# One gather per block: x, its gate and the dense output of a token share one row in DRAM

## The chip, the cores and the metric

The kernel runs on one core of a Trainium2 chip. The metric is the time of one execution on the device in microseconds (us). Five engines work side by side: TensorE (PE in the profile, its weight loads PEld), VectorE (DVE), ScalarE (ACT), GpSimd (POOL) and SyncE (SP), and 16 DMA engines move data for them.

## The reference

Two layers follow each other. The first is a block-sparse attention, the second a mixture of experts with a dense layer beside it.

```
# attention: 4 batches, 8 heads, 768 tokens, head size 64
k_min, k_max = min, max of k over chunks of 32 keys
ub   = sum(max(q*k_min, q*k_max));  causal chunks only
keep the 6 chunks with the highest ub for each query
x    = softmax(masked q k^T / 8) v          # -> 3072 tokens x 512
# experts: 8 of them, each with two 512 x 512 matrices
y_dense = relu(x @ w1_dense) @ w2_dense
logits  = x @ w_gate;  e = argmax(logits);  g = softmax(logits)[e]
out     = y_dense + g * (relu(x @ w1[e]) @ w2[e])
```

## The kernel before

**Attention, with the dense layer between.** The 16 pairs of heads (4 batches of 4 pairs) go through one after another. SP loads k, q and v three pairs ahead (`load`, L257), POOL casts them to f16, TensorE makes scores and the product with v, ACT the exponentials, POOL the masks on the diagonal. The result of a batch stands in `xbig`, in SBUF, as f16 rows of 528 elements for each token: 512 of x, two that hold the gate as one f32, and padding. When a batch is ready, its part of the dense layer (`batch_fills`, L172) is dealt out between the attention's steps of the next batch: `xtr` transposes x, `gate` (L185) makes the logits, the argmax and the gate's reciprocal sum and stores the batch's rows to the DRAM tensor `xd` (L206), `l1` and `l2` are the two layers, and `l2` stores 128 tokens of the dense output, as f32 rows of 2048 bytes, to the DRAM tensor `yd` (L231). Both stores are on SP's queue. The last batch's dense layer runs after the attention.

**Routing.** After the last gate the kernel computes for each token its place in a list sorted by expert (L446 to L509). The list is cut into 31 blocks of 128 places, each with one expert, and padded at the ends of experts. `gi` holds the token of each place for the gather, `si` the same for the scatter, with an index out of bounds for padding. The offset of each block's expert within the weights is loaded to TensorE's registers (L512).

**The expert stage.** A block goes through these steps:
- `gather(i)` (L520): POOL issues two indirect DMAs, 128 rows of `xd` (1056 bytes each) to the tile `xg`, and 128 rows of `yd` (2048 bytes each) to `yg`.
- `tx(i)` (L529): TensorE transposes x of the block (four 128 x 128 pieces), DVE copies the result to `exT`.
- `e1(i)` (L537): four matmuls with the expert's first matrix, ACT's relu to `eh`.
- `th(i)` (L546): four transposes of `eh`, ACT copies to `ehT`.
- `e2(i)` (L554): four matmuls with the second matrix; DVE makes `yo` = product x gate + dense output (L561), reading `xg` and `yg`; POOL issues an indirect DMA that scatters `yo` to the rows of `out` (L562).

`xg`, `yg` and `yo` come from the pool `eg` with three buffers each, so the gather of block i + 3 waits until the `yo` of block i has been computed, which is the last to read its `xg` and `yg`. Gathers are written two blocks ahead. A scatter writes to `out`, of which it isn't known which rows it hits, so each scatter waits until the one before it has landed. For the same reason a gather waits for every store to the tensor that it reads.

The order of instructions on each engine is fixed when the program is built, by a scheduler that works from the order in the source; each engine then takes its instructions in that order. The trace shows the order that came out: on POOL gather of x, gather of y, scatter, and on TensorE the second layer of a block in every other block split in two around the next `tx`.

Of the kernel before, what the change touches and what calls it, by code (L numbers as in the profile page):

```python
# [8 lines left out]
FP = mybir.dt.float32  # L9
BF = mybir.dt.bfloat16  # L10
HF = mybir.dt.float16
AF = mybir.ActivationFunctionType
ALU = mybir.AluOpType
# [4 lines left out]
def kernel(  # L18
# [12 lines left out]
    nc = tc.nc  # L31
    B, H, S, D = q.shape
    NT = S // 128
    NC = S // 32
    N, Dm = out.shape
# [6 lines left out]
    NP = B * HP  # L42
    NBLK = NM + E - 1
    XW = Dm + 16
    U16 = mybir.dt.uint16

    const = ctx.enter_context(tc.tile_pool(name="const", bufs=1))
    dram = ctx.enter_context(tc.tile_pool(name="dram", bufs=1, space=bass.MemoryType.DRAM))

    xd = dram.tile([N, XW], U16, name="xd")  # L50
    yd = dram.tile([N, Dm], FP, name="yd")

    ident = const.tile([128, 128], HF)
    make_identity(nc, ident)
# [55 lines left out]

    xbig = const.tile([128, NM, XW], HF)
    nc.gpsimd.memset(xbig[:, :, Dm:XW], 0.0)

# [30 lines left out]
    for u, un in enumerate(units):  # L144
        o = 0
# [13 lines left out]
    def evac(dst, src):  # L159
        evac_turn[0] += 1  # L160
        if evac_turn[0] % 2:
            nc.vector.tensor_copy(dst, src)
        else:
            nc.scalar.copy(dst, src)
# [3 lines left out]
    def ptile(kind, shape, dt, name):  # L168
        pool, tag = cur[kind]
        return pool.tile(shape, dt, name=name, tag=tag)  # L170

    def batch_fills(b):  # L172

        xT = mx.tile([128, NK, S], HF, name="xT")
        out_list = []

        def xtr(mi):
            def f():
                tp = ptile("tr", [128, NK, 128], HF, "tp")
                for ko in range(NK):  # L180
                    nc.tensor.transpose(tp[:, ko], xbig[:, b * NT + mi, ko * 128 : (ko + 1) * 128], ident)
                nc.vector.tensor_copy(xT[:, :, mi * 128 : (mi + 1) * 128], tp)
            return f

        def gate():  # L185
            lg = ptile("tr", [128, NT, E], FP, "lg")
            for mi in range(NT):
                for ko in range(NK):
                    nc.tensor.matmul(lg[:, mi], xT[:, ko, mi * 128 : (mi + 1) * 128], wg[:, ko],
                                     start=(ko == 0), stop=(ko == NK - 1))  # L190
            mxv = mg.tile([128, NT], FP, name="mxv")
            nc.vector.tensor_reduce(out=mxv, in_=lg, op=ALU.max, axis=mybir.AxisListType.X)
            dl = mg.tile([128, NT, E], FP, name="dl")
            nc.vector.tensor_tensor(dl, lg, mxv.unsqueeze(2).to_broadcast([128, NT, E]), ALU.subtract)
            el = mg.tile([128, NT, E], FP, name="el")
            nc.scalar.activation(el, dl, AF.Exp)
            cand = mg.tile([128, NT, E], FP, name="cand")
            nc.vector.scalar_tensor_tensor(cand, dl, 0.0, iom8, ALU.is_ge, ALU.mult)
            mn = mg.tile([128, NT], FP, name="mn")
            nc.vector.tensor_reduce(out=mn, in_=cand, op=ALU.min, axis=mybir.AxisListType.X)  # L200
            nc.vector.tensor_tensor(ohp[:, :, 1 + b * NT : 1 + (b + 1) * NT].rearrange("p e t -> p t e"),
                                    iom8, mn.unsqueeze(2).to_broadcast([128, NT, E]), ALU.is_equal)
            ss = mg.tile([128, NT, 1], FP, name="ss")
            nc.vector.tensor_reduce(out=ss, in_=el, op=ALU.add, axis=mybir.AxisListType.X)
            nc.vector.reciprocal(xbig[:, b * NT : (b + 1) * NT, Dm : Dm + 2].bitcast(FP), ss)
            nc.sync.dma_start(out=xd[b * S : (b + 1) * S].rearrange("(m p) w -> p m w", p=128),  # L206
                              in_=xbig[:, b * NT : (b + 1) * NT].bitcast(U16))

        G = 3

        def l1(g, j, hold):
            def f():
                if j == 0:
                    hold["h"] = mh.tile([128, NK, G * 128], HF, name="hT")
                hp = ptile("h", [128, G * 128], FP, "hp")
                for ko in range(NK):
                    nc.tensor.matmul(hp, wd[:, ko, j * 128 : (j + 1) * 128], xT[:, ko, g * G * 128 : (g + 1) * G * 128],  # L217
                                     start=(ko == 0), stop=(ko == NK - 1))
                nc.scalar.activation(hold["h"][:, j], hp, AF.Relu)  # L219
            return f  # L220

        def l2(g, i, hold):
            def f():
                yp = ptile("y", [128, Dm], FP, "yp")
                for j in range(NK):
                    nc.tensor.matmul(yp, hold["h"][:, j, i * 128 : (i + 1) * 128], wd[:, NK + j],  # L226
                                     start=(j == 0), stop=(j == NK - 1))
                ys = my.tile([128, Dm], FP, name="ys")
                evac(ys, yp)
                m = b * NT + g * G + i  # L230
                nc.sync.dma_start(out=yd[m * 128 : (m + 1) * 128], in_=ys)  # L231
            return f

        for mi in range(NT):
            out_list.append(xtr(mi))
        out_list.append(gate)
        dense = []
        for g in range(NT // G):
            hold = {}
            for j in range(NK):  # L240
                dense.append(l1(g, j, hold))
            for i in range(G):
                dense.append(l2(g, i, hold))
        return out_list, dense

    with (
# [10 lines left out]
        def load(p):  # L257
            b, hp = divmod(p, HP)
            for nm, src in (("k", k), ("q", q), ("v", v)):
                f = aload.tile([128, 2, NT, D], FP, name=nm + "f")  # L260
                st[p][nm] = f
                for g in range(2):
                    nc.sync.dma_start(out=f[:, g], in_=src[b, 2 * hp + g].rearrange("(t p) d -> p t d", p=128))

        def cast(p):
            s = st[p]
# [108 lines left out]
        for kind in ("tr", "h", "y"):  # L375
            cur[kind] = (pfill, "fb")
        load(0)
        load(1)
        load(2)
        load_dense()  # L380
# [15 lines left out]
        for i, (p, u) in enumerate(seq):  # L396
# [24 lines left out]
            if u == NU - 1:  # L421
                norm(p)
                if p % HP == HP - 1 and p + 1 < NP:
                    a, d = batch_fills(p // HP)
# [4 lines left out]
    with (  # L429
# [2 lines left out]
        tc.tile_pool(name="p3", bufs=2, space=bass.MemoryType.PSUM) as p3,  # L432
        tc.tile_pool(name="p4", bufs=1, space=bass.MemoryType.PSUM) as p4,
        tc.tile_pool(name="rt", bufs=1) as rt,
        tc.tile_pool(name="eg", bufs=3) as eg,
        tc.tile_pool(name="et", bufs=2) as et,
    ):
        cur.update(tr=(p1, "tr"), h=(p2, "h"), y=(p3, "y"))
# [2 lines left out]
        a, d = batch_fills(B - 1)  # L441
# [62 lines left out]
        gi = rt.tile([128, NBLK], mybir.dt.int32)  # L504
# [3 lines left out]
        si = rt.tile([128, NBLK], mybir.dt.int32)  # L508
# [10 lines left out]

        def gather(i):  # L520
            s = es[i]
            s["x"] = xg = eg.tile([128, XW], U16, name="xg")
            nc.gpsimd.indirect_dma_start(out=xg, out_offset=None, in_=xd,  # L523
                                         in_offset=bass.IndirectOffsetOnAxis(ap=gi[:, i : i + 1], axis=0))
            s["y"] = yg = eg.tile([128, Dm], FP, name="yg")
            nc.gpsimd.indirect_dma_start(out=yg, out_offset=None, in_=yd,  # L526
                                         in_offset=bass.IndirectOffsetOnAxis(ap=gi[:, i : i + 1], axis=0))

        def tx(i):  # L529
            s = es[i]  # L530
            tp = p1.tile([128, NK, 128], HF, name="tp", tag="tr")
            for ko in range(NK):
                nc.tensor.transpose(tp[:, ko], s["x"][:, ko * 128 : (ko + 1) * 128].bitcast(HF), ident)  # L533
            s["xT"] = xT = et.tile([128, NK, 128], HF, name="exT")
            nc.vector.tensor_copy(xT, tp)  # L535

# [17 lines left out]
        def e2(i):  # L554
            s = es[i]
            yp = p3.tile([128, Dm], FP, name="yp", tag="y")
            for j in range(NK):
                nc.tensor.matmul(yp, s["hT"][:, j], wef[:, bass.ds(offs[i] + (NK + j) * 512, 512)],  # L558
                                 start=(j == 0), stop=(j == NK - 1))
            o = eg.tile([128, Dm], FP, name="yo")  # L560
            nc.vector.scalar_tensor_tensor(o, yp, s["x"][:, Dm : Dm + 2].bitcast(FP), s["y"], ALU.mult, ALU.add)  # L561
            nc.gpsimd.indirect_dma_start(out=out, out_offset=bass.IndirectOffsetOnAxis(ap=si[:, i : i + 1], axis=0),  # L562
                                         in_=o, in_offset=None, bounds_check=N - 1, oob_is_err=False)

        gather(0)
        gather(1)
        tx(0)
        for i in range(NBLK):
            e1(i)
            if i + 2 < NBLK:  # L570
                gather(i + 2)
            if i + 1 < NBLK:
                tx(i + 1)
            if i > 0:
                e2(i - 1)
            th(i)
# [31 lines left out]
```

## Time and profile before

| what | value |
|---|---|
| time, median of 2 runs | 397.26 us (395.28 and 399.24) |
| profiled execution | 394.51 us, of which its span is 392.8 us |
| PE busy | 258.8 us, 66% of the span, 2426 matmuls |
| DVE, ACT busy | 192.1 us, 159.7 us |
| POOL busy | 208.0 us, 53% |
| DMA | 56.92 MB, mean 145 GB/s |

The span is the time from the first to the last instruction that the profiler recorded; the rest of the execution lies around it. A busy share over the whole span mixes the attention (up to about 235 us) with the expert stage, so the stages have to be read apart.

### The profile page before, as it was taken

The page shows a single profiled execution, that of the slowest core. Times are in us where ns is not written, and L with a number is a line of the kernel's source. Part 1 is how long each engine was busy: PE and PEld are TensorE (multiplying, and loading weights), DVE is VectorE, ACT ScalarE, POOL GpSimd, SP SyncE. Part 2 cuts the span into 40 slices and gives each one's busy share as a digit, 9 for nine tenths or more (in the row PEclk, how much of TensorE's full clock was granted, in tenths as well). Part 3 has the DMA queues.
Part 4 walks back from the last instruction along what each step waited for, and adds up shares of the span by engine and source line. Part 5 has one row for each costly group of instructions (what it writes and reads, how often), then busy time and mean ns, then how long its engine had stood idle before and what let it go on. Part 6 is the DMA issues. An engine that isn't in the chain of part 4 may idle for free. (4 is left out here: it accounts for less than half of the span.)

```text
span 392.8 us, 7052 instructions
## 1 busy us (share of the span) xinstructions
PE 258.8 (66%) x2426; PEld 152.8 (39%) x2426; DVE 192.1 (49%) x538; ACT 159.7 (41%) x303; POOL 208.0 (53%) x370
## 2 busy tenths in 40 slices
PE   0157377157599989999898872667555658565660
PEld 0135254045365666666665531333222323222230
DVE  8284438248387798777952890222222323232220
ACT  1016257056276867787675320322132222322230
POOL 9946185174455555554322025366756656666541
PEclk9998869779699999999999996888989996989895
DMA  9999999999997886211031425143444444444440
GB/s 182 208 222 214 208 204 198 170 199 204 222 236 191 190 200 145 94 53 56 3 119 49 164 106 173 42 154 114 131 133 132 149 145 135 134 136 133 128 121 0
DMA packets 98370, 56.92 MB, mean 145 GB/s; under 512 B 78462, under 2 KB 90750, under 8 KB 98336
## 3 DMA queue, kind: packets, MB, share of 16 engines
q1 hardware_dynamic: 81856, 28.42, 32.8%
q0 software_dynamic: 16480, 28.06, 30.1%
q8 instruction: 20, 0.33, 0.3%
q14 instruction: 14, 0.11, 0.1%
HBM read 50.08 MB, written 17.66 MB: 172 GB/s over the span
## 5 line engine op out<-in xcount | busy, mean ns | idle before, releaser
L334 ACT ACTIVATE ex<-sp 128x512 f16<-128x512 f32 (+1 forms) x176 | 91.7, 585 | 63.1 <-PE sp L330 31.1
L344 POOL TENSOR_SCALAR_AFFINE_SELECT ex<-ex 128x128 f16<-128x128 f16 (+1 forms) x176 | 52.2, 306 | 55.9 <-ACT ex L334 53.0
L362 PE MATMUL op<-v,ex 128*128 128x65 f16 x672 | 47.6, 200 | 34.6 <-POOL ex L344 29.7
L330 PE MATMUL sp<-r,kT 128*128 128x512 f16 (+3 forms) x256 | 65.1, 328 | 3.6 <-ACT ex L334 2.1
L362 PEld LDWEIGHTS <-ex 128*128 128x128 f16 x672 | 37.3, 101 | 49.5 <-POOL ex L344 35.0
L535 DVE COPY exT<-tp 128x512 f16<-128x512 f16 x31 | 13.2, 425 | 80.5 <-PE tp L533 59.3
L523 POOL DMA_INDIRECT xg<-xd,gi x31 | 30.3, 977 | 41.5 <-DVE yo L561 21.6
L552 ACT COPY ehT<-tp 128x512 f16<-128x512 f16 x31 | 18.2, 586 | 74.2 <-PE tp L550 67.9
L541 PE MATMUL hp<-we,exT 128*128 x124 | 37.4, 432 | 10.2 <-DVE exT L535 5.8
L558 PE MATMUL yp<-we,ehT 128*128 x124 | 38.8, 419 | 4.5 <-ACT ehT L552 2.6
L533 PE MATMUL tp<-ident,xg 128*128 128x128 f16 x124 | 14.2, 247 | 40.7 <-DMA xg<-xd,gi 40.7
L562 POOL DMA_INDIRECT out_dram<-yo,si x31 | 31.5, 1015 | 15.3 <-issue 13.4
L561 DVE SCALAR_TENSOR_TENSOR yo<-yp,xg,yg 128x512 f32<-128x512 f32 x31 | 23.3, 750 | 31.9 <-PE yp L558 27.2
L526 POOL DMA_INDIRECT yg<-yd,gi x31 | 29.4, 949 | 10.5 <-issue 10.2
L322 DVE COPY r<-pp 128x768 f16<-128x768 f16 x32 | 17.0, 554 | 32.8 <-PE pp L320 32.6
L544 ACT ACTIVATE eh<-hp 128x512 f16<-128x512 f32 x31 | 18.5, 597 | 35.2 <-PE hp L541 26.3
L533 PEld LDWEIGHTS <-xg 128*128 128x128 f16 x124 | 8.3, 108 | 56.9 <-DMA xg<-xd,gi 56.8
L217 PE MATMUL hp<-xT,wd 128*128 128x384 f16 x128 | 26.5, 325 | 0.7 <-ACT hT L219 0.3
L330 PEld LDWEIGHTS <-kT 128*128 128x128 f16 x256 | 21.8, 103 | 11.1 <-issue 8.2
L226 PE MATMUL yp<-wd,hT 128*128 128x512 f16 x96 | 24.6, 378 | 1.5 <-DVE xbig L371 1.0
L269 POOL CAST q<-qf 128x768 f16<-128x768 f32 x16 | 13.3, 831 | 21.5 <-DMA qf<-in_q_dram 20.9
L294 ACT ACTIVATE qp<-pp 128x768 f16<-128x768 f16 x16 | 13.0, 810 | 23.1 <-PE pp L292 23.1
(115 smaller groups left out, 431.0 us busy)
## 6 DMA issues: line engine op xcount, KB each, us to landing
we<-in_moe_w_dram POOLq DMA_DIRECT2D x16, 512.0 KB
kf<-in_k_dram SPq DMA_DIRECT2D x32, 192.0 KB, 4.4
qf<-in_q_dram SPq DMA_DIRECT2D x32, 192.0 KB, 4.5
vf<-in_v_dram SPq DMA_DIRECT2D x32, 192.0 KB, 4.7
yd<-ys SPq DMA_DIRECT2D x24, 256.0 KB, 2.1
xd<-xbig SPq DMA_DIRECT2D x4, 792.0 KB, 4.3
wd<-in_moe_w_dense_dram POOLq DMA_DIRECT2D x2, 512.0 KB
xg<-xd,gi POOLq DMA_INDIRECT x31
```

The costliest lines, as they stand in the source:

```text
L217: nc.tensor.matmul(hp, wd[:, ko, j * 128 : (j + 1) * 128], xT[:, ko, g * G * 128 : (g + 1) * G * 128], start=(ko == 0), stop=(ko == NK - 1))
L226: nc.tensor.matmul(yp, hold["h"][:, j, i * 128 : (i + 1) * 128], wd[:, NK + j], start=(j == 0), stop=(j == NK - 1))
L330: nc.tensor.matmul(sp[:, o : o + z - a], kT[p % NB][g][:, bb * 128 : (bb + 1) * 128], s["r", g][:, a:z], start=(o == 0), stop=True, skip_g ...
L334: nc.scalar.activation(ex[:, :o], sp[:, :o], AF.Exp, scale=0.125)
L344: nc.gpsimd.affine_select(out=exd, in_=exd, compare_op=ALU.is_ge, fill=0.0, base=0, pattern=[[0, n], [1, 128]], channel_multiplier=-1)
L362: nc.tensor.matmul(op[:, g, t * (D + 1) : (t + 1) * (D + 1)], ex[:, c : c + 128], v16[p % NB][:, g, bb, :], start=(u == g and n == 0), sto ...
L523: nc.gpsimd.indirect_dma_start(out=xg, out_offset=None, in_=xd, in_offset=bass.IndirectOffsetOnAxis(ap=gi[:, i : i + 1], axis=0))
L526: nc.gpsimd.indirect_dma_start(out=yg, out_offset=None, in_=yd, in_offset=bass.IndirectOffsetOnAxis(ap=gi[:, i : i + 1], axis=0))
L541: nc.tensor.matmul(hp, s["xT"][:, ko], wef[:, bass.ds(offs[i] + ko * 512, 512)], start=(ko == 0), stop=(ko == NK - 1))
L558: nc.tensor.matmul(yp, s["hT"][:, j], wef[:, bass.ds(offs[i] + (NK + j) * 512, 512)], start=(j == 0), stop=(j == NK - 1))
L561: nc.vector.scalar_tensor_tensor(o, yp, s["x"][:, Dm : Dm + 2].bitcast(FP), s["y"], ALU.mult, ALU.add)
L562: nc.gpsimd.indirect_dma_start(out=out, out_offset=bass.IndirectOffsetOnAxis(ap=si[:, i : i + 1], axis=0), in_=o, in_offset=None, bounds_c ...
```

## The change

The row of a token in `xd` grows to 3104 bytes: first 2048 bytes of the dense output as f32, then the 1056 bytes of x and gate as before. `yd` goes away: `l2` stores to the first part of `xd`'s rows, `gate` to the second. `gather` issues one indirect DMA per block for the whole row, and `tx` and the computation of `yo` read their parts of it. `eg` has four buffers in place of three, and gathers run three blocks ahead in place of two, with three before the loop. Each scatter is declared to be independent of the other scatters, so it no longer waits until the one before has landed. The loads of k, q and v take their pieces from a view over two heads; the elements and their number per DMA are the same.

```diff
+    RW = 2 * Dm + XW
-    xd = dram.tile([N, XW], U16, name="xd")
-    yd = dram.tile([N, Dm], FP, name="yd")
+    xd = dram.tile([N, RW], U16, name="xd")
...
-            nc.sync.dma_start(out=xd[b * S : (b + 1) * S].rearrange("(m p) w -> p m w", p=128),
+            nc.sync.dma_start(out=xd[b * S : (b + 1) * S, 2 * Dm :].rearrange("(m p) w -> p m w", p=128),
...
-                nc.sync.dma_start(out=yd[m * 128 : (m + 1) * 128], in_=ys)
+                nc.sync.dma_start(out=xd[m * 128 : (m + 1) * 128, 0 : 2 * Dm], in_=ys.bitcast(U16))
...
+                sv = src[b, 2 * hp : 2 * hp + 2].rearrange("g (t p) d -> p g t d", p=128)
                 for g in range(2):
-                    nc.sync.dma_start(out=f[:, g], in_=src[b, 2 * hp + g].rearrange("(t p) d -> p t d", p=128))
+                    nc.sync.dma_start(out=f[:, g], in_=sv[:, g])
...
-        tc.tile_pool(name="eg", bufs=3) as eg,
+        tc.tile_pool(name="eg", bufs=4) as eg,
...
-            s["x"] = xg = eg.tile([128, XW], U16, name="xg")
+            s["x"] = xg = eg.tile([128, RW], U16, name="xg")
             nc.gpsimd.indirect_dma_start(out=xg, out_offset=None, in_=xd,
-                                         in_offset=bass.IndirectOffsetOnAxis(ap=gi[:, i : i + 1], axis=0))
-            s["y"] = yg = eg.tile([128, Dm], FP, name="yg")
-            nc.gpsimd.indirect_dma_start(out=yg, out_offset=None, in_=yd,
                                          in_offset=bass.IndirectOffsetOnAxis(ap=gi[:, i : i + 1], axis=0))
...
-                nc.tensor.transpose(tp[:, ko], s["x"][:, ko * 128 : (ko + 1) * 128].bitcast(HF), ident)
+                nc.tensor.transpose(tp[:, ko], s["x"][:, 2 * Dm + ko * 128 : 2 * Dm + (ko + 1) * 128].bitcast(HF), ident)
...
-            nc.vector.scalar_tensor_tensor(o, yp, s["x"][:, Dm : Dm + 2].bitcast(FP), s["y"], ALU.mult, ALU.add)
-            nc.gpsimd.indirect_dma_start(out=out, out_offset=bass.IndirectOffsetOnAxis(ap=si[:, i : i + 1], axis=0),
+            nc.vector.scalar_tensor_tensor(o, yp, s["x"][:, 3 * Dm : 3 * Dm + 2].bitcast(FP), s["x"][:, 0 : 2 * Dm].bitcast(FP), ALU.mult, ALU.add)
+            sc = nc.gpsimd.indirect_dma_start(out=out, out_offset=bass.IndirectOffsetOnAxis(ap=si[:, i : i + 1], axis=0),
                                          in_=o, in_offset=None, bounds_check=N - 1, oob_is_err=False)
+            if i:
+                tc.declare_no_dep(sc.ins, group="scatter", reason="each scatter writes rows of its own")
+            tc.add_to_no_dep_group("scatter", sc.ins)
 
         gather(0)
         gather(1)
+        gather(2)
         tx(0)
         for i in range(NBLK):
             e1(i)
-            if i + 2 < NBLK:
-                gather(i + 2)
+            if i + 3 < NBLK:
+                gather(i + 3)
```

## Rows read from the trace of the kernel before

**Rows 1.** The page's part 2: busy tenths in 40 slices of 9.8 us, POOL.
```profile
POOL 9946185174455555554322025366756656666541
```

**Rows 2.** The windows: attention (0 to 210) and the expert stage (250 to 380).
```profile
0.00:210.00 210.00, 146.49 (x1766) 99.36 (x1767) 137.38 (x409) 114.44 (x223) 114.38 (x273) 0.93 0.85 167
...
250.00:380.00 130.00, 82.06 (x456) 37.66 (x454) 33.41 (x57) 33.53 (x57) 82.34 (x84) 0.91 0.43 135
```

**Rows 3.** Groups by line in 255 to 393 us, POOL's three.
```profile
L562 POOL DMA_INDIRECT out_dram<-yo,si x30 | 30.4, 1015 | 15.0 <-issue 13.1 <-DMA out_dram<-yo,si 1.9
L523 POOL DMA_INDIRECT xg<-xd,gi x27 | 26.3, 975 | 27.2 <-DVE yo L561 14.1 <-issue 6.2 <-DMA out_dram<-yo,si 4.5
L526 POOL DMA_INDIRECT yg<-yd,gi x27 | 25.6, 948 | 8.2 <-issue 7.9 <-DMA out_dram<-yo,si 0.3
```

**Rows 4.** The list of waits in 250 to 393 us: total, times, longest.
```profile
PE tp L533 <- DMA xg<-xd,gi: 36.5, 24, 2.6
...
POOL xg L523 <- DVE yo L561: 21.6, 9, 7.5
```

**Rows 5.** The tile yo: min/median/max ns, first and last start.
```profile
L561 DVE SCALAR_TENSOR_TENSOR yo<-yp,xg,yg x31: 742/751/753, 250.0 to 383.0; 128x512 f32<-128x512 f32 x31
```

**Rows 6.** The timeline in 254 to 275 us: start, duration, what, idle before.
```profile
254.50 0.40 PE L533 MATMUL tp<-ident,xg 128*128 128x128 f16 x4 [2.58 <-DMA xg<-xd,gi]
...
255.50 1.87 PE L541 MATMUL hp<-we,exT 128*128 x4 [0.38 <-DVE exT L535]
...
259.22 1.02 PE L541 MATMUL hp<-we,exT 128*128 x4
259.52 0.59 ACT L552 COPY ehT<-tp 128x512 f16<-128x512 f16 x1 [1.52 <-PE tp L550]
...
260.25 1.02 PE L558 MATMUL yp<-we,ehT 128*128 x4
...
261.31 0.75 DVE L561 SCALAR_TENSOR_TENSOR yo<-yp,xg,yg 128x512 f32<-128x512 f32 x1 [1.47 <-PE yp L558]
...
268.38 0.75 DVE L561 SCALAR_TENSOR_TENSOR yo<-yp,xg,yg 128x512 f32<-128x512 f32 x1 [0.43 <-issue]
...
269.40 0.98 POOL L523 DMA_INDIRECT xg<-xd,gi  x1 [1.88 <-DVE yo L561]
...
270.68 0.95 POOL L526 DMA_INDIRECT yg<-yd,gi  x1 [0.30 <-issue]
...
272.27 0.40 PE L533 MATMUL tp<-ident,xg 128*128 128x128 f16 x4 [1.66 <-DMA xg<-xd,gi]
...
272.50 0.39 PE L550 MATMUL tp<-ident,eh 128*128 128x128 f16 x4
...
273.27 1.02 PE L541 MATMUL hp<-we,exT 128*128 x4 [0.38 <-DVE exT L535]
...
274.39 0.60 ACT L544 ACTIVATE eh<-hp 128x512 f16<-128x512 f32 x1 [0.82 <-PE hp L541]
```

**Rows 7.** The timeline at the stage's start, 235 to 244 us.
```profile
235.14 1.06 POOL L523 DMA_INDIRECT xg<-xd,gi  x1 [6.20 <-PE yp L226]
235.25 1.06 SPq L231 DMA_DIRECT2D yd<-ys  x2
...
238.62 0.61 PE L533 MATMUL tp<-ident,xg 128*128 128x128 f16 x4 [3.31 <-DMA xg<-xd,gi]
...
240.08 0.96 POOL L526 DMA_INDIRECT yg<-yd,gi  x1 [1.32 <-issue]
...
243.92 3.57 PE L541 MATMUL hp<-we,exT 128*128 x8 [3.26 <-issue]
```

**Rows 8.** The line L512 on TensorE's queue: the load of the experts' offsets.
```profile
L512 PEldq TENSOR_LOAD <-eo x1: 2802/2802/2802, 240.9 to 240.9; - x1
```

**Rows 9.** The timeline at the end, 383 to 393 us.
```profile
383.00 0.75 DVE L561 SCALAR_TENSOR_TENSOR yo<-yp,xg,yg 128x512 f32<-128x512 f32 x1 [1.31 <-PE yp L558]
...
386.37 0.98 POOL L562 DMA_INDIRECT out_dram<-yo,si  x1 [1.88 <-issue]
```

## The prediction

> **What bounds the kernel now.** I read the share of busy time over the span first [rows 1], to cut it into stages. Up to about 235 us the attention and the dense layer run; there POOL's digits fall to nearly nothing and then stand at 5 to 7 until the end. The windows [rows 2] put numbers to this: in 250 to 380 us POOL is busy 82.3 of 130 us, TensorE 82.1, DVE and ACT 33 each, and the DMA engines 43% at 135 GB/s. No engine is full, so the stage waits in a circle, and the change lies in this circle alone.
>
> The rate first: the 31 `yo` run from 250.0 to 383.0 us [rows 5], so a block costs 133.0 / 30 = 4.43 us. POOL's groups [rows 3] say what it does with that: gathers of xg 0.975, of yg 0.948, scatter 1.015 us, each behind 0.30 us between two issues of POOL [rows 6]: 3 x 0.30 + 2.94 = 3.84 us of 4.43. The list of waits [rows 4] names the rest. TensorE waits 36.5 us for xg to land, and the gather of xg waits 21.6 us for `yo`, which frees its buffer. So two limits lie close together: POOL's queue (3.84 us) and the loop through three buffers. I worked this loop out from the timeline [rows 6]: `yo` ends at 269.13, the gather starts at 269.40 and takes 0.98, its rows are used by `tx` at 272.27 (1.89 us later), `tx` to the end of `eh` is 274.99 - 272.27 = 2.72 us, then a handover of about 0.2, `th` 0.39, another 0.2, and from `ehT` to the end of `yo` 262.06 - 259.52 = 2.54. In all 0.27 + 0.98 + 1.89 + 6.05 = 9.19 us. Three blocks share one turn: 3 x 4.43 = 13.3 us. The other 4.1 us of the turn are POOL's and TensorE's queues and the slow clock.
>
> The clock belongs to it: the first layer of a block takes 1.87 us after TensorE idled 2.58 us, and 1.02 us in other blocks [rows 6], the two levels of 1.2 and 2.4 GHz; over the stretch the granted clock is 0.91 [rows 2]. Each long wait for a gather is thus paid again in slow matmuls.
>
> **The change part by part.**
>
> *One gather for two.* POOL loses one instruction per block. The trace has no gather of 3104-byte rows, so its price is bounded: 1056-byte rows cost 0.975, 2048-byte rows 0.948 [rows 3], so the price doesn't grow with the row, and I take 0.98. The upper bound is the two together with their gap, 2.22, if a longer row were to be issued as two pieces; lower than 0.95 I see no reason for. POOL per block then: 0.98 + 1.015 + 0.60 = 2.59 us (upper bound 3.84 as now).
>
> *Landing.* The bytes don't change: 128 x (3104 + 2048) = 660 KB per block. At 135 GB/s the engines are 43% busy, which makes some 314 GB/s if they were full, 2.1 us per block: no bound at any rate that I forecast. But `tx` must now wait for all of the row, 262 KB more, an estimate of 262 / 314 = 0.83 us, at best nothing, when both parts overlap in flight. The Trainium skill (DMA: Bandwidth & Descriptors, section Anatomy of one DMA, SWDGE path) gives 2.0 us plus the bytes over 436 GB/s for a DMA of this kind. By that the merged gather takes 2.91 us against 2.31 for xg alone, 0.6 us more instead of 0.83; for xg the rows have 2.87 us from the start of the issue to the use (269.40 to 272.27, [rows 6]), so the page's size is about right here. By the page the turn below would be 0.2 us shorter, 0.06 us per block.
>
> *Four buffers instead of three,* and a gather three blocks ahead. The turn becomes 9.19 + 0.83 = 10.02 us over four blocks: 2.5 us per block with no queueing, and 14.1 / 4 = 3.5 with all the 4.1 us of today's. The most of these hang on the cause that goes (xg behind yg and a scatter in POOL's queue, the slow clock), so this isn't the likeliest end.
>
> *TensorE.* With its data there and the fast clock, a block is `tx` and `th` together 0.62 us (272.27 to 272.89), 1.02 for each layer: 2.66 us, plus the 0.38 us in which the first layer waits for `exT` [rows 6] where nothing lies between: 3.04. That is above POOL's 2.59 and the loop's 2.5. So TensorE becomes late next. I take 3.1 us per block, bounds 2.66 (no gap left) and 3.54 (the loop with today's queueing). If the clock fell as now, 10% of 2.66 come on top, and this lies within these bounds.
>
> *Scatters that don't wait for each other.* POOL's wait of this kind shows at the end: the last `yo` is done at 383.75, and its scatter starts at 386.37 [rows 9], where 0.3 after `yo` would do: 2.3 us saved. In the middle of the stage two scatters are 4.4 us apart and the wait is over in time; at 3.1 us it would begin to bind (1.0 us of issue and 1.9 of waiting between the last two make 2.9), so this part keeps the way free rather than gaining: nothing more counted, 0.3 us per block if it should still wait.
>
> *The start.* Now xg needs only `xd`, and its first gather starts at 235.14 us; yg had to wait for the last store of the dense output and starts at 240.08 [rows 7]. The merged gather needs that store: 4.94 us later. POOL does nothing else then. Behind it are `tx`, the load of the experts' offsets on TensorE's queue (2.80 us, [rows 8]) and the first layer at 243.92. If the order stays, all moves by 4.94 and the longer landing, and the first `yo` is at 250.0 + 5.5 = 255.5. If the load slips ahead of `tx`, where TensorE idles, 2.8 us and some handing over come back: 251.6. I take 255.5.
>
> *Stores and loads.* 24 stores of the dense output (one per 128 tokens) and 4 of x (one per batch) go to the same tensor, rows 3104 bytes apart; bytes, number and issuing queue (SP) stay. The loads' new view reads the same elements. In the 210 us of attention [rows 2] I change nothing. If a store were slower by a half, only the last one is on the path: 1 us.
>
> **The sum,** against the profiled execution: first `yo` 255.5 + 30 x 3.1 = 348.5; from the last `yo` to the end 392.8 - 383.0 - 2.3 = 7.5; span 356.0; with the 1.7 us around the span (394.51 - 392.8) 357.7 us, so 358. The profiled execution lies 0.7% under the median of the two runs shown, 397.26, and near the lower one, 395.28. Two per cent, some 8 us, is about what a measurement tells from no change.
>
> **Rivals.**
>
> *TensorE at its floor* (0.08): 2.66 us and an early start: 251.6 + 79.8 + 7.5 + 1.7 = 341 us, to about 345. For it: DVE and ACT are a quarter busy. Against: the order of the instructions is fixed ahead, and the 0.38 us gap shows in it.
>
> *The merged gather costs POOL as much as two* (0.10): 3.84 us per block, 255.5 + 115.2 + 9.2 = 380 us. For it: no row has a gather of over 2048 bytes. Against: doubling the row cost POOL nothing [rows 3].
>
> *Nothing gained* (0.08): the turn was bound by TensorE's order and slow clock, not by buffers, and what POOL saves becomes idle: 4.3 us per block, 255.5 + 129 + 9.2 = 394 us. For it: TensorE is as busy as POOL in the stage [rows 2]. Against: its longest waits are for xg [rows 4].
>
> *Slower* (0.04): x and the dense output now interleave in one tensor, and if their stores were held to follow each other, each of the 24 on SP's queue would wait for the landing of the one before, and the loads of k, q and v queue behind them. The last store was issued by 236.3 [rows 7] and let yg go by 240.08, up to 4 us for one landing; 24 x 2 to 4 us is 50 to 100 us of a blocked queue. It ends slower from the point where more than 1.9 us per store isn't covered by the lead of three head pairs (the forecast's gain, 394.5 - 358 = 36.5, plus 8, over 24); at 2.1 us uncovered 358 + 50 = 408 us. Against: the two stores at 235.25 go out within 1.06 us [rows 7], so stores of different rows don't wait for each other.
>
> **How the numbers follow.** The forecast, 2.9 to 3.54 us per block, has 0.70, and spans 349 to 371 us. The range reaches from 344 to 380: up for the gather's price and the 0.7% between the profile and the median, down for an early start; this leaves out some 0.2. Faster by over 2%: 0.70 + 0.10 + 0.08 = 0.88. Within: 0.08. Slower: 0.04.
>
> **What would show it.** POOL has two instructions per block, a gather near 1 us; `yo` come every 3.1 us; the waits of `tx` for the gather and of the gather for `yo` shrink to a few us; the granted clock in the stage goes to 0.95 or more; the first gather starts near 240 us; the last scatter starts 0.3 us after the last `yo`. It is wrong if the gather takes near 2 us, if `tx` waits for it in each block although POOL idles (the landing, not the issue, is long), or if SP's stores come apart by a landing.

## The result, and the profile after

The changed kernel takes 356.16 us (median of 355.44 and 356.88) against 397.26 before: 0.897 times, with an interval of 0.876 to 0.917. The forecast was 358. The profiled execution has a span of 355.1 us.

The page's part 2 for the kernel after, POOL and the granted clock in 40 slices of 8.9 us, against [rows 1]:

```profile
POOL 9976248237445455545543240104166566556543
PEclk9999858968969999999999999995699999999998
```

The expert stage begins with POOL's 4 in slice 28 (the first gathers), so it lasts 13 slices of 8.9 us, where it was 16 of 9.8. In these 13 the clock's digits are low only at the first two: 5 in the slice in which TensorE waits for the first gather and the load of the offsets, 6 in the next; from then on they are 9 or 8.

The windows after, attention and a part of the expert stage (us; busy time of PE, PEld, DVE, ACT, POOL with counts; granted clock; DMA share; GB/s):

```profile
0.00:210.00 210.00, 146.52 (x1758) 99.08 (x1759) 137.60 (x409) 113.86 (x222) 114.23 (x272) 0.93 0.86 167
...
280.00:310.00 30.00, 22.75 (x148) 11.48 (x147) 10.03 (x18) 11.24 (x19) 18.36 (x19) 1.00 0.60 194
```

The attention is the same as in [rows 2], 146.5 us of TensorE in 210, DMA 0.86 and 167 GB/s: no cost of the stores to one tensor shows there. In the stage the clock is 1.00 and the DMA engines move 194 GB/s where it was 135; POOL is busy 18.4 of 30 us.

POOL's two groups after, in 255 to 355 us (busy, mean ns | idle before, releasers), against the three of [rows 3]:

```profile
L561 POOL DMA_INDIRECT out_dram<-yo,si x31 | 31.5, 1016 | 14.2 <-issue 8.2 <-DVE yo L560 6.0
L525 POOL DMA_INDIRECT xg<-xd,gi x27 | 26.4, 977 | 35.2 <-DVE yo L560 28.1 <-issue 6.0 <-DVE exT L534 1.1
```

A gather of 3104-byte rows costs POOL 0.977 us, as much as one of 1056 (0.975). The waits after, in 250 to 355 us (total, times, longest), against [rows 4]:

```profile
POOL xg L525 <- DVE yo L560: 28.1, 16, 11.0
...
PE tp L532 <- DMA xg<-xd,gi: 11.0, 17, 1.2
```

11.0 of the 28.1 us is one wait before the first `yo`, so 17.1 us over 30 blocks is left; TensorE's wait for gathers fell from 36.5 to 11.0 us. The tile `yo` after (ns, first and last start), with its scatters, against [rows 5]:

```profile
L560 DVE SCALAR_TENSOR_TENSOR yo<-yp,xg x31: 741/744/752, 254.8 to 350.1; 128x512 f32<-128x512 f32 x31
L561 POOL DMA_INDIRECT out_dram<-yo,si x31: 983/1019/1038, 257.1 to 351.1; - x31
```

(350.1 - 254.8) / 30 = 3.18 us per block, where it was 4.43. The timeline at the stage's start after (start, duration, what, idle before), against [rows 7]:

```profile
239.93 1.06 POOL L525 DMA_INDIRECT xg<-xd,gi  x1 [10.03 <-issue]
...
243.87 0.61 PE L532 MATMUL tp<-ident,xg 128*128 128x128 f16 x4 [7.92 <-DMA xg<-xd,gi]
...
248.50 1.87 PE L540 MATMUL hp<-we,exT 128*128 x4 [4.03 <-issue]
```

The first gather starts at 239.93 (forecast 240.08), the first layer at 248.50 where it was 243.92, behind the load of the experts' offsets, which here runs from 245.5 to 248.3. At the end the last scatter starts at 351.1 (above), 0.3 us after the last `yo` ends at 350.8, where it was 2.6 [rows 9]; the span ends 5.0 us after the last `yo` begins, where it was 9.8. Against the sum: start 0.7 us earlier, blocks 30 x 0.08 = 2.4 us longer, end 2.5 us shorter.

### The profile page after: what moved, and what is told of

Read it like the earlier page. It is cut to its first block, busy times and chain, and to the rows that moved or that the text cites. A ratio compares the mean times of both kernels' runs of the same rounds, so it can differ in the third digit from the quotient of the medians.

```text
span 355.1 us, 6966 instructions
## 1 busy us (share of the span) xinstructions
PE 247.8 (70%) x2426; PEld 150.3 (42%) x2426; DVE 190.9 (54%) x538; ACT 160.1 (45%) x303; POOL 179.1 (50%) x339
## 3 DMA queue, kind: packets, MB, share of 16 engines
q1 hardware_dynamic: 81856, 28.42, 36.5%
## 4 chain that ended last, share of the span: by engine, by line
issue 21%; PE 21%; POOL 17%; DVE 15%; DMA 13%; ACT 3%; SPq 3%; POOLq 1%; ACTq 0%; DVEq 0%
DMA qf<-in_q_dram 12%; POOL out_dram L561 8%; PE sp L332 4%; PE hp L218 4%; PE yp L227 4%; POOL xg L525 4%; SPq L265 3%; PE op L364 2%; ACT ex L336 2%; DVE ks L282 2%; DVE ks L283 2%; POOL ex L346 2%; PE pp L322 2%; POOL we L127 1%; DVE kT L288 1%
## 5 line engine op out<-in xcount | busy, mean ns | idle before, releaser
L364 PE MATMUL op<-v,ex 128*128 128x65 f16 x672 | 47.4, 199 | 34.3 <-POOL ex L346 29.6
L525 POOL DMA_INDIRECT xg<-xd,gi x31 | 30.3, 979 | 46.1 <-DVE yo L560 28.1
L540 PE MATMUL hp<-we,exT 128*128 x124 | 33.5, 393 | 12.5 <-DVE exT L534 7.8
L557 PE MATMUL yp<-we,ehT 128*128 x124 | 36.4, 380 | 1.9 <-ACT ehT L551 1.1
L532 PE MATMUL tp<-ident,xg 128*128 128x128 f16 x124 | 12.9, 230 | 19.3 <-DMA xg<-xd,gi 18.9
L560 DVE SCALAR_TENSOR_TENSOR yo<-yp,xg 128x512 f32<-128x512 f32 x31 | 23.1, 746 | 3.9 <-PE yp L557 3.8
L271 POOL CAST q<-qf 128x768 f16<-128x768 f32 x16 | 13.3, 831 | 19.9 <-DMA qf<-in_q_dram 19.4
L220 ACT ACTIVATE hT<-hp 128x384 f16<-128x384 f32 x32 | 15.9, 496 | 13.0 <-PE hp L218 12.6
```

The lines of the kernel that those rows point to most:

```text
L364: nc.tensor.matmul(op[:, g, t * (D + 1) : (t + 1) * (D + 1)], ex[:, c : c + 128], v16[p % NB][:, g, bb, :], start=(u == g and n == 0), sto ...
L532: nc.tensor.transpose(tp[:, ko], s["x"][:, 2 * Dm + ko * 128 : 2 * Dm + (ko + 1) * 128].bitcast(HF), ident)
L540: nc.tensor.matmul(hp, s["xT"][:, ko], wef[:, bass.ds(offs[i] + ko * 512, 512)], start=(ko == 0), stop=(ko == NK - 1))
L560: nc.vector.scalar_tensor_tensor(o, yp, s["x"][:, 3 * Dm : 3 * Dm + 2].bitcast(FP), s["x"][:, 0 : 2 * Dm].bitcast(FP), ALU.mult, ALU.add)
```

## The experiments

The change has three parts: **A**, one gather for two; **B**, four buffers and a gather three blocks ahead; **C**, scatters that don't wait. The runs were made in three sets; the kernels of one set ran on one chip, where the kernel before took 393.94, 396.30 and 395.18 us; on which chip the two kernels of the section on the result ran (397.26 and 356.16 us) isn't on record. "Per block" is the distance of the `yo` as above, from one profiled execution of each run.

```
set  run                        parts      time    ratio to before (95%)    per block
1    e3_merge_alone             A          399.98  1.017 (1.010 to 1.023)   4.56
1    e2_three_buffers           A + C      397.49  1.011 (1.003 to 1.019)   4.57
1    e1_waits_kept              A + B      367.25  0.933 (0.927 to 0.940)   3.33
1    e6_all_but_merge           B + C      369.34  0.938 (0.932 to 0.945)   3.68
2    e4_four_buffers_alone      B          400.99  1.011 (1.007 to 1.015)   4.38
2    e5_no_wait_alone           C          393.33  0.995 (0.992 to 0.998)   4.43
2    e7_x_alone                 B + C, x   349.84  0.882 (0.878 to 0.886)   3.10
2    e8_five_buffers            A + B + C  355.57  0.898 (0.893 to 0.904)   3.13
3    e9_four_buffers_again      B          400.36  1.014 (1.009 to 1.018)   4.40
3    e10_all_but_merge_again    B + C      390.95  0.989 (0.981 to 0.997)   4.33
3    e11_after_again            A + B + C  352.86  0.892 (0.889 to 0.895)   3.08
3    e12_offsets_early          A + B + C  352.75  0.895 (0.889 to 0.901)   3.04
```

My theory was the prediction's: merging relieves POOL, the buffers shorten the turn, and the dropped waits only keep the way free. The rivals, run by run, were that another part carries the gain.

**The waits kept (A + B).** Against the kernel after:

```diff
-            if i:
-                tc.declare_no_dep(sc.ins, group="scatter", reason="each scatter writes rows of its own")
-            tc.add_to_no_dep_group("scatter", sc.ins)
```

> The changed kernel, but each scatter waits again until the one before has landed. Theory (merge and buffers carry the gain; the wait binds only from about 2.9 us per block): blocks stay near 3.2 us, only the end grows by about 2 us: 358 to 361 us. Rival (the waits between scatters held POOL's queue, and to drop them is the main part): blocks go to 3.7 us or more, 372 us or more.

It took 367.25 us, between the two. The waits of POOL (250 to 366 us), POOL's timeline in 301 to 310 us, and the tile `yo` with its scatters:

```profile
POOL out_dram L561 <- DMA out_dram<-yo,si: 24.2, 19, 2.9
```

```profile
301.73 1.02 POOL L561 DMA_INDIRECT out_dram<-yo,si  x1 [0.55 <-DMA out_dram<-yo,si]
...
303.05 0.98 POOL L525 DMA_INDIRECT xg<-xd,gi  x1 [0.30 <-issue]
...
305.02 1.02 POOL L561 DMA_INDIRECT out_dram<-yo,si  x1 [0.99 <-DMA out_dram<-yo,si]
...
308.31 1.02 POOL L561 DMA_INDIRECT out_dram<-yo,si  x1 [1.00 <-DMA out_dram<-yo,si]
```

```profile
L560 DVE SCALAR_TENSOR_TENSOR yo<-yp,xg x31: 740/750/753, 254.8 to 354.8; 128x512 f32<-128x512 f32 x31
L561 POOL DMA_INDIRECT out_dram<-yo,si x31: 982/1017/1038, 257.1 to 364.6; - x31
```

These three scatters wait for the one before to land and come 3.29 us apart. From the end of one (302.75) to the start of the next (305.02) it is 2.27 us, where the forecast had 1.9 from [rows 9]. The last scatter starts 9.8 us after the last `yo`, so POOL lags behind: 3.58 us per scatter against 3.33 per `yo`. The wait binds in the stage, and costs some 11 us against the kernel after (356.16, not in this set), not the 2.3 that the forecast counted. Most of it shows behind the last `yo`: the span ends 13.8 us after it begins, where the kernel after has 5.0.

**Three buffers kept (A + C).** Against the kernel after:

```diff
-        tc.tile_pool(name="eg", bufs=4) as eg,
+        tc.tile_pool(name="eg", bufs=3) as eg,
-        gather(2)
-            if i + 3 < NBLK:
-                gather(i + 3)
+            if i + 2 < NBLK:
+                gather(i + 2)
```

> The changed kernel with three buffers and gathers two blocks ahead. Theory (the loop from one yo over the gather to a later yo is about 10 us without queueing, and three blocks must hold it): 3.7 to 4.0 us per block, TensorE waits for the gather in each block and its clock falls in part: 372 to 381 us. Rival (the queue of POOL alone was the bound, and it is short now): 3.2 us per block, 356 us.

397.49 us: worse than both, no gain at all. Its waits (250 to 393 us), a stretch of the timeline, and the tile `yo`:

```profile
POOL xg L525 <- DVE yo L560: 70.9, 14, 11.9
```

```profile
301.18 0.75 DVE L560 SCALAR_TENSOR_TENSOR yo<-yp,xg 128x512 f32<-128x512 f32 x1
...
302.20 0.97 POOL L525 DMA_INDIRECT xg<-xd,gi  x1 [4.68 <-DVE yo L560]
302.43 0.60 ACT L543 ACTIVATE eh<-hp 128x512 f16<-128x512 f32 x1 [0.39 <-PE hp L540]
303.25 0.75 DVE L560 SCALAR_TENSOR_TENSOR yo<-yp,xg 128x512 f32<-128x512 f32 x1 [1.31 <-PE yp L557]
...
306.13 0.40 PE L532 MATMUL tp<-ident,xg 128*128 128x128 f16 x4 [2.92 <-DMA xg<-xd,gi]
306.36 0.39 PE L549 MATMUL tp<-ident,eh 128*128 128x128 f16 x4
...
310.94 0.75 DVE L560 SCALAR_TENSOR_TENSOR yo<-yp,xg 128x512 f32<-128x512 f32 x1 [0.43 <-PE yp L557]
...
311.95 0.98 POOL L525 DMA_INDIRECT xg<-xd,gi  x1 [4.85 <-DVE yo L560]
```

```profile
L560 DVE SCALAR_TENSOR_TENSOR yo<-yp,xg x31: 749/751/752, 254.3 to 391.5; 128x512 f32<-128x512 f32 x31
```

POOL does a gather and a scatter where it did three DMAs, and its wait for `yo` grew from 21.6 us [rows 4] to 70.9: what POOL saves becomes waiting. `yo` ends at 301.93, the gather starts at 302.20, and its rows are used at 306.13: 3.93 us from issue to use, where `xg` alone took 2.87 [rows 6]. Three buffers give a turn of 3 x 4.57 = 13.7 us, before it was 13.3.

What fills the turn stands on TensorE's queue, whose order is fixed. The `eh` of a block is done at 303.03, but its `th` stands behind the `tx` of the next block, which waits for its gather until 306.13, so `th` starts at 306.36, 3.33 us late. The `yo` of this block starts at 310.94 and lets the gather of 311.95 go. From gather to gather this turn takes 9.75 us and moves on by two blocks, not three: `yo` come in pairs, 2.07 us apart (301.18, 303.25) and then 7.69 (310.94). No run has `th` ahead of `tx`, so what this order costs isn't shown by an experiment.

**The merge alone (A).** Both edits above together.

> One gather per block alone: three buffers, two blocks ahead, scatters that wait. Theory: as with three buffers above, plus 2 us at the end: 374 to 385 us. Rival (the merge brings nothing without the buffers, the loop stays 4.4 us per block, and the later start costs 5 us): 398 to 402 us.

399.98 us, the rival's number; the tile `yo`:

```profile
L560 DVE SCALAR_TENSOR_TENSOR yo<-yp,xg x31: 749/751/752, 254.2 to 390.9; 128x512 f32<-128x512 f32 x31
```

4.56 us per block, as in A + C. With three buffers the merged gather is worth nothing on POOL and costs 4 us more at the start: the kernel gets 1.7% slower.

**All but the merge (B + C).** Against the kernel before:

```diff
-        tc.tile_pool(name="eg", bufs=3) as eg,
+        tc.tile_pool(name="eg", bufs=4) as eg,
...
+        gather(2)
-            if i + 2 < NBLK:
-                gather(i + 2)
+            if i + 3 < NBLK:
+                gather(i + 3)
...
+            if i:
+                tc.declare_no_dep(sc.ins, group="scatter", reason="each scatter writes rows of its own")
+            tc.add_to_no_dep_group("scatter", sc.ins)
```

> The kernel before with four buffers, gathers three blocks ahead and scatters that don't wait for each other, but still two gathers per block. Theory (POOL issues three DMAs in 3.84 us per block and becomes the bound): 3.84 to 4.0 us per block, first yo near 250, so 374 to 381 us. Rival (the buffers alone were the bound): 3.2 us per block, 352 us.

369.34 us, nearer to the theory. One turn of POOL on the timeline, and the tile `yo`:

```profile
297.49 0.99 POOL L523 DMA_INDIRECT xg<-xd,gi  x1 [0.30 <-DVE exT L535]
...
298.78 0.94 POOL L526 DMA_INDIRECT yg<-yd,gi  x1 [0.31 <-issue]
...
300.02 1.02 POOL L562 DMA_INDIRECT out_dram<-yo,si  x1 [0.30 <-issue]
...
301.35 0.97 POOL L523 DMA_INDIRECT xg<-xd,gi  x1 [0.30 <-DVE exT L535]
```

```profile
L561 DVE SCALAR_TENSOR_TENSOR yo<-yp,xg,yg x31: 750/751/752, 250.2 to 360.7; 128x512 f32<-128x512 f32 x31
```

POOL issues without a pause, 0.30 us between any two, and a block takes 301.35 - 297.49 = 3.86 us. That is the forecast's 3 x 0.30 + 2.94 = 3.84, seen as the bound. The mean of 3.68 is lower; four blocks are gathered before the first `yo`, which gives a head start. So here POOL's queue is what the merge takes away.

**Four buffers alone (B):** the last diff without its last hunk.

> The kernel before with four buffers and gathers three blocks ahead, nothing else. Theory as it now stands (the loop through three buffers was the bound; with four of them POOL's three issues per block are, 3.86 us): the scatters' wait ends before POOL comes to the next scatter, since two gathers lie between, so 369 to 373 us, as with the waits dropped. Rival (the wait for the scatter before binds as it did with one gather per block): 380 us or more.

400.99 us, 1% slower than before; the rival was right in sign. I took from it that the waits of scatters might carry 30 us (401.0 against 369.3), and repeated both kernels on one chip, with the kernel after.

> Four buffers alone once more, now on one chip with the version that also drops the waits. In its first run 7 copies by DVE and ACT began up to 2 to 3 us after TensorE had written what they read, which the other set of runs, made on another chip, didn't show. Theory A (the waits between scatters cost these 30 us): 399 to 401 us again, and 369 us for the version without waits. Theory B (the chip of that set of runs did): both versions come close to each other, at 369 to 375 us on a chip without the late starts.

> Two gathers, four buffers, no waits between scatters, once more, on the same chip as four buffers alone. Theory A: 369 us. Theory B: on a chip with late starts 385 us or more, on one without 369 us and four buffers alone with it.

> The changed kernel once more, for the times of all versions on one chip: 355 to 357 us. If late starts are in its time (it had some in its profile), a chip without them gives 345 to 350 us.

B took 400.36 again, but B + C took 390.95, where the same program took 369.34 in set 1. So the 30 us fall: on one chip the dropped waits are worth 9.4 us beside B, most of it at the end (from the last `yo` to the end of the span 16.1 us in e9, 7.5 in e10). On that chip A then brings 390.95 to 352.86. The 21.6 us between two runs of one program are the last section's.

**The dropped waits alone (C):** the last hunk of that diff on the kernel before.

> The kernel before with scatters that don't wait for each other, nothing else. Theory: scatters are 4.4 us apart, the wait is over in time, only 2 to 3 us at the end are saved: 390 to 393 us beside 394. Rival (the waits hold POOL's queue here too): 385 us or less.

393.33 us, 0.995 times, as expected. `yo` run from 249.9 to 382.9 us, 4.43 per block as before; only the end is shorter (7.5 us from the last `yo`, before 9.8).

**The bytes.** B + C without the gather of the dense output; a tile of zeros is read in its place:

```diff
-            s["y"] = yg = eg.tile([128, Dm], FP, name="yg")
-            nc.gpsimd.indirect_dma_start(out=yg, out_offset=None, in_=yd,
-                                         in_offset=bass.IndirectOffsetOnAxis(ap=gi[:, i : i + 1], axis=0))
+            s["y"] = yz
```

> One gather per block of 1056-byte rows with x and gate, four buffers, three ahead, no wait between scatters; the dense output isn't gathered, a tile of zeros is added in its place, so the dense part is missing from the output. It tells what the 2048 bytes more in the merged row cost. Theory (the merged gather lands 1 us later and starts 4.7 us later, and TensorE waits for it): first yo near 250, 2.9 to 3.0 us per block, 343 to 347 us. Rival (bytes and landing don't matter once there are four buffers): 3.18 us per block and only the earlier start, 351 us.

349.84 us. The tile `yo`, and TensorE's wait for the gather (250 to 345 us):

```profile
L562 DVE SCALAR_TENSOR_TENSOR yo<-yp,xg,yz x31: 750/751/752, 251.0 to 344.0; 128x512 f32<-128x512 f32 x31
```

```profile
PE tp L534 <- DMA xg<-xd,gi: 14.6, 18, 1.8
```

3.10 us per block with a third of the row's bytes, 3.08 and 3.18 with all of them (e11, after). No price of the 2048 bytes per block shows here. But e11 is of another chip, and e7 has more late starts (last section), so a price of some tenths of a us isn't ruled out. What e7 gains is its start: first `yo` at 251.0 against 254.8.

**A fifth buffer.** The kernel after with `bufs=5` and a gather four blocks ahead.

> The changed kernel with five buffers and gathers four blocks ahead. Theory (the loop through four buffers still binds in part, as POOL waits 28 us for yo and TensorE 11 us for gathers): 2.95 to 3.1 us per block, 349 to 353 us. Rival (TensorE's own order and handovers set the 3.18 us): 356 us as the changed kernel.

355.57 us, no gain, as the rival had it, but not for its reason. The tile `yo`, and two blocks on the timeline:

```profile
L560 DVE SCALAR_TENSOR_TENSOR yo<-yp,xg x31: 742/751/753, 253.7 to 347.6; 128x512 f32<-128x512 f32 x31
```

```profile
318.55 0.75 DVE L560 SCALAR_TENSOR_TENSOR yo<-yp,xg 128x512 f32<-128x512 f32 x1 [0.44 <-PE yp L557]
318.57 1.03 PE L540 MATMUL hp<-we,exT 128*128 x4
...
319.43 0.39 PE L532 MATMUL tp<-ident,xg 128*128 128x128 f16 x4
...
320.72 0.75 DVE L560 SCALAR_TENSOR_TENSOR yo<-yp,xg 128x512 f32<-128x512 f32 x1 [0.44 <-PE yp L557]
```

Where nothing waits, `yo` come 320.72 - 318.55 = 2.17 us apart. A layer holds TensorE for 0.86 us (318.57 to 319.43), not for the 1.02 that its group lasts: the next group starts before the modelled end of this one. So 3.13 us isn't TensorE's floor. In this run eight single blocks take 4.3 to 5.6 us; the last section shows what holds them.

**The load of offsets earlier.** `tx(0)` placed behind the load on TensorE's queue:

```diff
-        tx(0)
+        with tc.issue_after(loads[-1].ins):
+            tx(0)
```

> The changed kernel with the load of the experts' offsets put ahead of the first transposes on TensorE's queue, where TensorE idles until the first gather has landed. Theory (the load's 2.8 us stand on the path between the first tx and the first layer): first yo 3 us earlier, 3 us less than the changed kernel on the same chip. Rival (the blocks that follow wait for their gathers anyway, so the head start is lost): no difference.

352.75 us, the same as e11. Its waits on TensorE's queue and the load, the start on the timeline, and the waits and `yo` of the stage:

```profile
L514 PEldq EVENT_SEMAPHORE  x5: 51/51/51, 242.6 to 243.1; - x5
L514 PEldq TENSOR_LOAD <-eo x1: 2788/2788/2788, 243.2 to 243.2; - x1
```

```profile
242.65 0.10 PEld L532 LDWEIGHTS <-xg 128*128 128x128 f16 x1 [8.63 <-DMA xg<-xd,gi]
...
246.00 0.58 PE L532 MATMUL tp<-ident,xg 128*128 128x128 f16 x4 [11.47 <-issue]
...
247.18 1.87 PE L540 MATMUL hp<-we,exT 128*128 x4 [0.60 <-DVE exT L534]
```

```profile
POOL xg L525 <- DVE yo L560: 25.8, 17, 11.0
```

```profile
L560 DVE SCALAR_TENSOR_TENSOR yo<-yp,xg x31: 741/744/751, 253.4 to 344.7; 128x512 f32<-128x512 f32 x31
```

The transposes start where the load ends, at 246.00, so the load is ahead of them now. But it starts at 243.2, behind five waits that begin at 242.6, in the moment in which the first weight load of `tx` starts after 8.63 us of waiting for the gather. To go by these times, that weight load still stands ahead of the load, and TensorE's queue idles for the gather as before. The path is 1.3 us shorter (first layer at 247.18 instead of 248.50), and the price of the load stays untested.

## Why the prediction was right, and where it was not

**The bound.** That two limits lie close together, POOL's queue and the turn through the buffers, was right, and the runs show each alone. A + C takes POOL's work and leaves the turn: 4.57 us. With three buffers it is the rival *Nothing gained* that came: what POOL saves becomes idle, and TensorE's order is part of the turn. B + C lengthens the lead and leaves POOL's work: 3.86 us, POOL without a pause. What the forecast didn't draw from it: lifting one limit can be worth little or nothing. A and B alone make the kernel 1 to 1.7% slower; A + B, and on one chip B + C, gain 6 to 7%. B alone was run only in sets 2 and 3, with many late starts both times (last section); what it brings without them isn't shown.

**One gather for two.** The price was right, 0.977 us where I took 0.98. As a share of the gain it was told wrongly, as the change's main relief. Its worth hangs on B: nothing with three buffers, 38 us on the chip of set 3, and 369.34 - 356.16 = 13 us between two sets of runs where B + C ran at 369.

**Landing.** The term was 0.83 us; 3.93 - 2.87 = 1.06 was measured (e2). By the figures of the Trainium skill (DMA: Bandwidth & Descriptors, section Anatomy of one DMA, SWDGE path) it is an estimate of 0.6 us more; the trace is above both, and the measurement decides. No price of it per block shows with four buffers (e7), as far as runs on different chips can tell.

**Four buffers.** The turn was put at 10.02 us without queueing and up to 14.1 with today's. With the landing as measured it is 9.19 + 1.06 = 10.25 us without; 4 x 3.18 = 12.7 was measured. So 2.5 us of the 4.1 us of queueing stayed. One term of the turn was sized too small: the "handover of about 0.2" from `eh` to `th`. In the kernel before, at the `tx` from which the forecast took its turn:

```profile
269.76 0.60 ACT L544 ACTIVATE eh<-hp 128x512 f16<-128x512 f32 x1 [0.31 <-PE hp L541]
```

This `eh` is done at 270.36, and its `th` starts at 272.50, right behind the `tx` that waited for the next block's gather [rows 6]: 2.14 us. From the timelines, as a mean over blocks 3 to 30, it is 1.8 us before, 2.2 in A + C and 0.7 in the kernel after. So `yo` of a block can hang on the gather of the next, and the turn then covers fewer blocks than there are buffers.

**TensorE.** This step failed, though its number, 3.1 us, came out: "TensorE becomes late next", at 2.66 us of work and 0.38 of a gap. Groups of matmuls were added up by durations that overlap, and the gap was added on top: a layer holds TensorE for 0.86 us, not 1.02 (e8). Blocks that wait for nothing take 2.17 us (e8), less than POOL's 2.59. What stands at 3.18 us is POOL's 2.59 us and the 17.1 us that it still waits for `yo`, 0.57 per block: 3.16. For e12 it is 2.59 + (25.8 - 11.0) / 30 = 3.08, and 3.04 was measured. This sum tells where the time shows, not what sets it. It does show that the circle of POOL, buffers and TensorE's order went on: the waits didn't shrink to the "few us" that were to show the forecast right, but to 17.1 us for `yo` and 11.0 for gathers. The right number came from a wrong term, which is luck. The rival of 341 us, with TensorE at its floor, was likewise built on 2.66.

**The clock.** It came back as foretold, 1.00 in 280 to 310 us, and A + C, without the gain, has 0.84 in 280 to 340 us.

**Scatters.** Mis-sized: "nothing more counted" for the stage, 2.3 us at the end. Without C, A + B is some 11 us slower than the kernel after. The point from which it binds, 2.9 us, was near the block's 3.1; beside gathers it is 3.3 (e1), past it. The fallback price that I named, 0.3 us per block, 9 us, is near the 11; POOL's scatters come 3.58 - 3.13 = 0.45 us further apart without C.

**The start** was right: the first gather at 239.93 us (forecast 240.08), the first `yo` at 254.8 (255.5). **Stores and loads** cost nothing that shows, so the rival on the slow side had no ground: the last two stores go out at 235.89 within 1.06 us, as before.

**The end** was 2.5 us shorter than the sum. The three drains of POOL's queue at the end, after and before (min/median/max ns, first and last start):

```profile
L607 POOLq DRAIN  x3: 51/103/3411, 350.9 to 354.8; - x3
```

```profile
L603 POOLq DRAIN  x3: 51/103/5853, 386.1 to 392.5; - x3
```

The longest shrank from 5.85 to 3.41 us. In all runs with one gather per block and C the span ends 5.0 to 5.1 us after the last `yo`, with two gathers and C 7.5 (e5, e6, e10). That the drain hangs on the number of DMAs (93 before, 62 after) is argued from these two numbers and wasn't tried.

So the total came out by misses that nearly cancel: the blocks by 2.4 us up, the start and the end by 3.2 down, and under the blocks a floor that isn't there. One slip in the spans changes nothing: 2.9 us per block makes 255.5 + 87 + 9.2 = 352 us, not 349.

## What to carry to other kernels

Where two limits lie close together, price a change that lifts both as one thing; a part alone can bring nothing, or a loss, as A did here. For a loop through buffers, compare the turn (from issue to the read that frees the buffer) with buffers times period, and follow the fixed order on each engine: a step that stands behind another block's wait makes the turn cover fewer blocks than there are buffers. For an engine's floor take distances from start to start where nothing waits, not sums of durations, which overlap. Wait lists show where a saving went: here what POOL saved under three buffers came back as its own wait for `yo`.

## What the runs showed that I had not expected

One program, B + C, took 369.34 us on one chip and 390.95 on another, where the kernel before differs by 0.3%. What differs on the timelines is that much of what follows TensorE starts late; the granted clock is lower too, 0.86 against 0.93 over the span, and which of the two comes first isn't shown. First e10, then e6, the same program:

```profile
280.86 0.40 PE L533 MATMUL tp<-ident,xg 128*128 128x128 f16 x4 [1.33 <-DMA xg<-xd,gi]
...
281.96 0.40 PE L550 MATMUL tp<-ident,eh 128*128 128x128 f16 x4
...
284.05 0.42 DVE L535 COPY exT<-tp 128x512 f16<-128x512 f16 x1 [4.82 <-remote]
...
286.97 0.59 ACT L552 COPY ehT<-tp 128x512 f16<-128x512 f16 x1 [5.07 <-PE tp L533]
```

```profile
294.43 0.39 PE L550 MATMUL tp<-ident,eh 128*128 128x128 f16 x4
...
294.91 0.59 ACT L552 COPY ehT<-tp 128x512 f16<-128x512 f16 x1 [1.80 <-PE tp L550]
```

In e10 the transposes of `eh` end at 282.36, and the copy that needs nothing else starts at 286.97; `exT` starts 2.8 us after its transposes. In e6 the copy follows 0.09 us after the end. Of 31 copies to `ehT`, counted on the timelines, 11 begin more than 1 us late in e10 (34.3 us in all), 11 in e4 (27.7), 10 in e9 (30.0), 7 in e7 (10.3), 5 in e8 (12.3), 4 in the kernel after (5.0), 3 in e11 (4.1), 1 in e12 (1.2), 1 in before (1.6); in e1, e2, e3, e5 and e6 none. (The expectation of e9 above names 7 for e4, which is too few.) The chip alone isn't it: e4 and e5 ran on one chip. ACT and DVE are held alike, while POOL goes on issuing. In e8 it is such starts that break the row of 2.17 us: a copy to `exT` at 311.05 is 4.0 us late, and the block takes 5.36 us. The records of TensorE's ends are modelled, so the work itself may be late; the cause stays open. The kernel after wasn't run in set 1, so how much of the merge's 38 us in set 3 is POOL's queue and how much these late starts can't be told closer than by the estimate: 30 x (3.68 - 3.18) = 15 us for the blocks, less 4.6 for the later first `yo`, plus 2.5 at the end, 13 us.
